# Two rows of 16 small-tile matmuls of a pair of batches formed as one row of 32, in a fused attention and mixture-of-experts kernel

## The chip, the cores and the metric

The kernel runs on one core of one Trainium2 chip. The metric is device time in microseconds of the whole launch, the median of several runs. Beside the runs there is one profiled execution, from which all views of the trace come.

## What is computed

There are 8 batches of 576 tokens with 8 heads of 64, 32 packed queries per head, 4 experts, a model width of 512 and a hidden width of 1024 per expert.

```python
p_packed = sm_attn(p, k, v)                      # 32 packed rows per head
out = sm_attn(q, p_packed, p_packed)             # tokens attend to the packed rows
x = out.transpose(0, 2, 1, 3).reshape(B * S, H * D)
for e in range(E):
    h = np.maximum(x @ w1[e], 0.0)
    result += prob[:, e:e + 1] * (h @ w2[e])     # prob: normalised domain probabilities
```

`sm_attn` is softmax attention with the scale 1/8.

## The kernel before

**Folding.** The attention output of a token is a weighted sum of 32 packed rows per head. So `x @ w1` is computed as (attention weights of the tokens) x (packed rows times `w1`). The second factor is the folded weight of a batch. A *chunk* is half an expert's hidden width (512 columns); there are 8 chunks. `g_form` (L286) folds a chunk for a pair of batches: its matmuls multiply `ppbd` (packed rows, 64x32) with `wraw` (the raw `w1`, 64x512) on small tiles of TensorE, which write different partitions of the same PSUM buffer. The four pairs of heads go as two *groups* g = 0, 1. One group of a pair of batches is 8 calls, which the trace shows as a row of 16 records on L76. `together` keeps such calls side by side in TensorE's queue. One PSUM buffer (`dbl`, two banks) takes one group: the first half for the even batch, the second for the odd one. Each half is then split in two parts of the tile `ghl`: ACT casts it to the high part (`hi_of`, L105), DVE subtracts that from PSUM for the low part (`lo_of`, L109).

**Units.** The main loop runs over 64 *units* u = (sweep, chunk, batch): 4 sweeps over pairs of batches, 8 chunks in each, two batches. (The second and third units change places, as do the two before the last.) So an even unit works on the even batch of a pair, an odd unit on the odd one, and each sweep has 16 units. A unit does seven *products* (`product`, L452: 12 matmuls `dbl<-st,tt`, a Strassen-like scheme for `h @ w2`), i = 0 to 6. Between them stand, behind i = 1, 3, 4 and 6 (the table `GROUPS`), the four groups of 12 matmuls with `ghl` (`mm1_groups`: `dbl<-xh,ghl` and `dbl<-xl,ghl`), which compute a quarter each of the next unit's hidden blocks. Their result leaves PSUM through DVE (L343, `ablk`). `s_operand` makes the Strassen sums of the blocks on DVE (L368, `sblk`) and splits them into `st` on ACT (L105) and POOL (L109). A product's result is added to `acc` by DVE (L470); in the first chunk ACT copies it (L468).

**Folding within the units.** An even unit u from 4 to 60 folds the *next* chunk for both batches of the pair. `g_form` is a generator: one step makes one group, and `next(gsteps, None)` is called behind products 3 and 6; in unit 60 (`AHEAD`) behind products 0 and 1. Units 0 to 3 fold in other ways; unit 3 already issues both groups without anything between. The raw weights of the chunk after are loaded behind an even unit (`w1_load`, four tiles `wraw`, four buffers).

**Other work.** In each sweep but the last the attention of the next pair (`pack_unit`, `tok_unit`: L172 to L269, among them `ppn`, L208) is cut into steps and laid between the products. In the first sweep, and only there, `t_form` also makes the seven Strassen operands `tt` of `w2` for the next chunk, with differences on POOL and DVE (L405, tiles `b` and `ablk`), and stores them. Later sweeps load `tt` back.

**Buffers.** PSUM has four buffers `dbl` for everything. `ghl` has five buffers in `gpool`; from the second sweep on the pool `glast` holds one more tile (`ghl6`), used once.

**What sets the order.** TensorE's order is that of the code within limits: a row that `together` makes stays whole, and matmuls before and after it don't cross it. All else, the order of each engine's queue and which buffer a tile gets, is decided by a scheduler that simulates the program. Each engine works through its queue in order, so an instruction that waits holds up all behind it.

Of the kernel before, what the change touches and what calls it, by code (L numbers as in the profile page):

```python
# [9 lines left out]
F32R = mybir.dt.float32r  # L10
# [6 lines left out]
P = 128  # L17
B, H, S, D = 8, 8, 576, 64
NPK = 32
E, DM, F = 4, 512, 1024  # L20
NPAIR = H // 2
NG = NPAIR // 2
SB = B // 2
HS = S // 2
FC = 512
NCH = E * F // FC
# [14 lines left out]
def attention_moe(ctx: ExitStack, tc: tile.TileContext, q, k, v, p, dp, w1, w2, out):  # L41
    nc = tc.nc
# [7 lines left out]
    gpool = pool("gpool")  # L50
# [33 lines left out]
    def dbl():  # L84
        return ps_dbl.tile([P, 2, 512], F32, name="dbl")
# [12 lines left out]
    def cols(b, hh):  # L98

        i = (hh + b) % 2  # L100
        return slice(i * NPK, (i + 1) * NPK)

    def hi_of(dst, src, eng):
        if eng is nc.scalar:
            return nc.scalar.copy(out=dst, in_=src)  # L105
        return eng.tensor_copy(out=dst, in_=src)

    def lo_of(dst, src, hi, eng):
        return eng.tensor_tensor(out=dst, in0=src, in1=hi.bitcast(F32), op=ALU.subtract)  # L109
# [173 lines left out]

    gs = {}

    def g_form(bs, ch, raws):  # L286

        for g in range(NG):
            ps = dbl()
            pss = {b: ps[:, b % 2] for b in bs}  # L290
            calls = []
            for hs in range(4):
                pr, hh = 2 * g + hs // 2, hs % 2
                rows = slice(hh * D, (hh + 1) * D)
                for b in bs:
                    c0 = (hs // 2) * 2 * NPK + cols(b, hh).start
                    calls.append(dict(
                        out=pss[b][c0:c0 + NPK, :], lhsT=ppbd[b % 4][rows, pr, cols(b, hh)], rhs=raws[pr][rows, :],
                        start=True, stop=True,
                    ))  # L300
            together(calls)
            for b in bs:
                if (b, ch, g) == (B - 1, NCH - 2, 0):
                    ghl = glast.tile([P, 2, FC], F32R, name="ghl6")
                else:
                    ghl = gpool.tile([P, 2, FC], F32R, name="ghl", bufs=5)
                hi_of(ghl[:, 0, :], pss[b], nc.scalar)
                marks[b, ch, g, "low"] = lo_of(ghl[:, 1, :], pss[b], ghl[:, 0, :], nc.vector).ins
                gs.setdefault((b, ch), []).append(ghl)
            yield  # L310

    units = [(sb, ch, 2 * sb + i) for sb in range(SB) for ch in range(NCH) for i in range(2)]
# [271 lines left out]
    nothing = iter(())  # L584
    GROUPS = {1: ((0, 0),), 3: ((0, 1),), 4: ((1, 1),), 6: ((1, 0),)}
    GROUPS_LAST = {1: ((0, 0),), 3: ((1, 0),), 4: ((0, 1),), 6: ((1, 1),)}
    GROUPS_LATE = {4: ((0, 0), (0, 1)), 5: ((1, 1),), 6: ((1, 0),)}
    AT_FIRST = ((4, pack_unit, 0), (7, pack_unit, 1), (9, tok_unit, 0), (12, tok_unit, 1))
    def second_tile(n):
# [16 lines left out]
    for u, (sb, ch, b) in enumerate(units):  # L606
        odd = b % 2 == 1
        nxt = units[u + 1] if u + 1 < len(units) else None

        step = 2 * ch + b % 2  # L610
        if sb + 1 < SB:
            pair = [2 * sb + 2, 2 * sb + 3]
            for at_step, make, g in AT_FIRST if sb == 0 else AT_LATER:
                if at_step == step:
                    drain(back)
                    back = make(pair, g, att_tile, relief=sb == 0)

        gsteps = nothing
        nsb, nch = (sb, ch + 1) if ch + 1 < NCH else (sb + 1, 0)
        if u == 0:  # L620
            gsteps = g_form([0], 1, raws)
        elif u == 2 or u == 3:
            gsteps = g_form([1] if u == 2 else [0, 1], u - 1, raws)
            drain(gsteps)
            raws = w1_load(u)
        elif 3 < u <= AHEAD and not odd and nsb < SB:
            gsteps = g_form([2 * nsb, 2 * nsb + 1], nch, raws)
        if u == 2 * NCH - 1:
            later.close()
            glast = later.enter_context(tc.tile_pool(name="glast", bufs=1, reuse_waits="tile"))  # L630
        elif u == LAST - 1:
            extra = plain_operand(NCH - 1)
            next(extra)
        elif u == LAST:
            for _ in combine(b, SUMS_LAST):
                pass
            for r in range(2):
                for n in range(2):
                    quadrant(r, n)
                    if r == 0:  # L640
                        s_operand(u, LA + n)
            break
        forming = u == 0 or u > 2 and odd and sb == 0 and ch + 1 < NCH
        if forming:
            tsteps = t_form(ch + 1, raw_tile, {"t1": nc.gpsimd, "t2": nc.vector, "t3": nc.vector, "t4": nc.gpsimd})
            next(tsteps)
        for i in range(NPROD):
            product(u, i)
            n = i + LA
            if n < NPROD:  # L650
                s_operand(u, n)
            elif nxt:
                s_operand(u + 1, n - NPROD)
            if nxt:
                for grp in (GROUPS_LATE if u in (1, AHEAD) else GROUPS_LAST if u == LAST - 1 else GROUPS).get(i, ()):
                    mm1_groups(u + 1, [grp])
            if u == 0:
                drain(gsteps)
            elif i in ((0, 1) if u == AHEAD else (3, 6)):
                next(gsteps, None)  # L660
            if u == 1 and i == 3:
                drain(second)
                drain(g_form([1], 0, raws))
                raws = w1_load(1)
            for _ in range(SECOND[u][i] if u in SECOND and i < len(SECOND[u]) else 0):
                next(second, None)
            if i == 4 and u > 1 and u + 2 < len(units) and units[u + 2][1] % 2 == 0:
                load_probs(units[u + 2][2], units[u + 2][1] // 2)
            if i % 2 == 0 or sb == 0 and step >= AT_FIRST[2][0]:
                next(back, None)  # L670
            if sb == 0 and i in (FORM_ODD if odd or u == 0 else FORM_EVEN):
                next(tsteps, None)
            next(sums, None)
            if sb == 0 and not odd:
                t_store(ch, i)
            if u == LAST - 1:
                if i == 1:
                    next(extra)
                elif i in (0, 5, 6):
                    t_load(nxt[1], i)  # L680
            elif nxt and not forming and nxt[1] != ch:
                t_load(nxt[1], i)
        drain(gsteps)
        drain(sums)
        if ch == NCH - 1:
            sums = combine(b, SUMS)
        if u == 0:
            raws = w1_load(0)
            load_probs(1, 0)
        elif not odd and u > 2:  # L690
            nsb, nch = (sb, ch + 2) if ch + 2 < NCH else (sb + 1, ch + 2 - NCH)
            if nsb < SB:
                raws = w1_load(nch)
# [34 lines left out]
```

## Time and profile before

| what | us |
| --- | --- |
| median of 3 runs | 1298.41 (1297.54 to 1298.51) |
| the profiled execution's own time | 1297.59 |
| its span in the trace | 1295.8 |
| first sweep with units 4 to 15, about | 120 to 360 |
| later three sweeps and the end, about | 360 to 1296 |

The engines are PE (TensorE's matmuls), PEld (its weight loads), DVE (VectorE), ACT (ScalarE), POOL (GpSimd) and SP (SyncE, which issues DMAs). A timeline row gives start and length in us, engine, line, operation, `out<-in` by the program's names, shapes, the number of instructions of the row, and in brackets the idle time ahead of it with what ended it. Matmuls are pipelined: a matmul starts while its predecessors still run, so lengths overlap and the time that PE's stream takes is read from start to start.

### The profile page before, as it was taken

To read this page: it belongs to the slowest core of one execution; us is meant where nothing else is said; L and a number is where in the kernel's file an instruction comes from. 1 tells how busy PE (TensorE), PEld (TensorE's weight loads), DVE (VectorE), ACT (ScalarE), POOL (GpSimd) and SP (SyncE) were. 2 spreads that over 40 slices of the span, in tenths; PEclk is the share of its full clock that TensorE was granted. 3 is DMA by queue.
4 is the path that set the end of the run, shared out by engine and by line. 5 is a ranking of instruction groups with operands and counts; after the bars stand their busy time and mean duration, and the time that the engine had idled before them with its cause. 6 is when DMAs were issued, how large, how long until landed. Compare 5 with 4: busy or idle time off the path is not lost.

```text
span 1295.8 us, 26890 instructions
## 1 busy us (share of the span) xinstructions
PE 1273.2 (98%) x10776; PEld 1178.4 (91%) x10776; DVE 951.5 (73%) x1304; ACT 495.2 (38%) x884; POOL 857.0 (66%) x570
## 2 busy tenths in 40 slices
PE   7899999999999999999999999999999999999998
PEld 4689999998999989999999999999999999999998
DVE  6786677899975666997686666789669466666676
ACT  3445545646334333333325433333333533333321
POOL 4778888798995544666577554476568655555565
PEclk9999999999999999999999999999999999999999
DMA  9885656544465543554444456433446443344562
GB/s 350 305 300 191 219 169 230 180 145 167 157 220 195 170 154 119 175 177 156 134 149 168 162 163 205 144 126 105 148 141 210 155 138 111 115 139 151 169 205 97
DMA packets 91707, 223.93 MB, mean 173 GB/s; under 512 B 9280, under 2 KB 32192, under 8 KB 91584
## 3 DMA queue, kind: packets, MB, share of 16 engines
q1 hardware_dynamic: 90768, 221.92, 51.4%
q8 instruction: 86, 1.41, 0.4%
q10 hardware_dynamic: 816, 0.30, 0.1%
q14 instruction: 37, 0.30, 0.1%
HBM read 183.31 MB, written 38.87 MB: 171 GB/s over the span
## 4 chain that ended last, share of the span: by engine, by line
PE 84%; POOL 7%; DVE 5%; issue 2%; DMA 1%; ACT 1%; SPq 0%; DVEq 0%; ACTq 0%; POOLq 0%
PE dbl L68 77%; PE dbl L76 6%; POOL st L109 4%; POOL tt L109 2%; DVE sblk L368 1%; POOL b L405 1%; PE dbl L71 1%; DMA xl<-in_q 1%; POOL acc L501 1%; DVE ablk L343 1%; DVE nb L172 0%; DVE a L264 0%; DVE acc L470 0%; ACT a L178 0%; POOL xl L109 0%
## 5 line engine op out<-in xcount | busy, mean ns | idle before, releaser
L68 PEld LDWEIGHTS dbl<-st,tt 128*128 128x128 f32 x5388 | 729.3, 188 | 59.2 <-POOL st L109 25.7
L68 PE MATMUL dbl<-st,tt 128*128 128x288 f32 x5388 | 773.4, 297 | 2.8 <-POOL st L109 1.9
L109 POOL TENSOR_TENSOR st<-sblk,st 128x576 fp32r<-128x576 f32 x252 | 392.5, 1565 | 204.6 <-ACT st L105 198.2
L68 PE MATMUL dbl<-xh,ghl 128*128 128x288 f32 x2048 | 416.7, 295 | 5.0 <-DVE ghl L109 2.7
L109 POOL TENSOR_TENSOR st<-ablk,st 128x576 fp32r<-128x576 f32 x193 | 289.7, 1505 | 181.4 <-ACT st L105 171.3
L470 DVE TENSOR_TENSOR acc<-dbl,acc 128x576 f32<-128x576 f32 x385 | 289.1, 753 | 115.6 <-PE dbl L68 114.6
L68 PEld LDWEIGHTS dbl<-xh,ghl 128*128 128x128 f32 x2048 | 328.4, 188 | 7.5 <-DVE ghl L109 4.1
L343 DVE SCALAR_TENSOR_TENSOR ablk<-dbl,pbt 128x576 f32<-128x576 f32 x256 | 192.5, 753 | 158.2 <-PE dbl L68 157.7
L68 PE MATMUL dbl<-xl,ghl 128*128 128x288 f32 x1024 | 300.9, 294 | 1.0 <-DVE xl L109 1.0
L105 ACT CAST st<-sblk 128x576 fp32r<-128x576 f32 x252 | 170.5, 677 | 283.5 <-DVE sblk L368 194.6
L105 ACT CAST st<-ablk 128x576 fp32r<-128x576 f32 x193 | 130.6, 677 | 224.3 <-PE dbl L68 202.3
L68 PEld LDWEIGHTS dbl<-xl,ghl 128*128 128x128 f32 x1024 | 192.1, 188 | 1.4 <-DVE xl L109 1.4
L105 ACT CAST ghl<-dbl 128x512 fp32r<-128x512 f32 x128 | 74.9, 587 | 146.5 <-PE dbl L76 87.8
L368 DVE TENSOR_TENSOR sblk<-ablk 128x576 f32<-128x576 f32 x126 | 122.0, 969 | 9.3
L109 DVE TENSOR_TENSOR ghl<-dbl,ghl 128x512 fp32r<-128x512 f32 x128 | 87.4, 685 | 11.1 <-ACT ghl L105 7.5
L76 PE MATMUL dbl<-wraw,ppbd 64*32 64x512 f32 x1024 | 74.7, 601 | 0.4 <-DMA wraw<-in_w 0.4
L368 DVE TENSOR_TENSOR sblk<-ablk,sblk 128x576 f32<-128x576 f32 x63 | 67.0, 1063 | 5.7
L109 POOL TENSOR_TENSOR tt<-b,tt 128x512 fp32r<-128x512 f32 x42 | 62.3, 1491 | 2.1 <-ACT tt L105 2.0
L368 DVE TENSOR_TENSOR sblk<-sblk,ablk 128x576 f32<-128x576 f32 x63 | 57.1, 907 | 1.7
L501 POOL TENSOR_TENSOR acc<-acc,acc 128x576 f32<-128x576 f32 x28 | 47.0, 1688 | 16.2 <-DVE acc L470 16.1
L468 ACT COPY acc<-dbl 128x576 f32<-128x576 f32 x56 | 35.9, 642 | 41.6 <-PE dbl L68 41.0
L501 DVE TENSOR_TENSOR acc<-acc,acc 128x576 f32<-128x576 f32 x28 | 40.8, 1462 | 5.0 <-POOL acc L501 4.6
(91 smaller groups left out, 433.2 us busy)
## 6 DMA issues: line engine op xcount, KB each, us to landing
tt<-td SPq DMA_DIRECT2D x192, 512.0 KB, 4.4
wraw<-in_w SPq DMA_DIRECT2D x136, 256.0 KB, 3.1
td<-tt SPq DMA_DIRECT2D x56, 512.0 KB, 3.7
pbt<-pnd SPq DMA_DIRECT2D x32, 288.0 KB, 4.4
out<-acc SPq DMA_DIRECT2D x31, 288.0 KB, 2.3
kt<-in_k SPq DMA_DIRECT2D x14, 576.0 KB, 5.7
kt<-in_q SPq DMA_DIRECT2D x14, 576.0 KB, 5.5
vt<-in_v SPq DMA_DIRECT2D x15, 512.0 KB, 5.6
```

The lines of the kernel that those rows point to most:

```text
L68: on_pe(nc.tensor.matmul(**kw))
L71: on_pe(nc.tensor.transpose(**kw))
L76: ins = nc.tensor.matmul(**kw).ins
L105: return nc.scalar.copy(out=dst, in_=src)
L109: return eng.tensor_tensor(out=dst, in0=src, in1=hi.bitcast(F32), op=ALU.subtract)
L343: nc.vector.scalar_tensor_tensor(out=a, in0=ps[:, :, 0:HS], scalar=0.0, in1=pbt[b][:, c * HS:(c + 1) * HS].rearrange("p (o t) -> p o t", o ...
L368: nc.vector.tensor_tensor(out=t, in0=blk(x), in1=blk(y), op=op)
L405: eng[m].tensor_tensor(out=blk[place], in0=blk[x], in1=blk[y], op=ALU.subtract)
L468: nc.scalar.copy(out=accs[b, i], in_=psv)
L470: nc.vector.tensor_tensor(out=accs[b, i], in0=psv, in1=accs[b, i], op=ALU.add)
L501: eng.tensor_tensor(out=m[dst], in0=m[x], in1=m[y], op=op)
```

## The change

`g_form` takes a list of groups of folding groups. In even units from 4 on, both groups go as one step: 16 calls (32 records) side by side, over two PSUM buffers, and only then the four evictions. In the first sweep the step stands behind product 6, where the `ghl` tiles of the chunk before have had their last use, so that five buffers do; the first group of the odd units there moves from behind product 1 to behind product 2 (`GROUPS_ODD`). In the later sweeps it stands behind product 3 and takes its tiles from a ring of six (`ghl_tile`, every sixth from `glast`). In unit 60 it stands behind product 0.

```diff
+    def ghl_tile():
+        n, ring["n"] = ring["n"], ring["n"] + 1
+        if n % 6 == 0:
+            return glast.tile([P, 2, FC], F32R, name="ghl6")
+        return gpool.tile([P, 2, FC], F32R, name="ghl", bufs=5)
+
+    def g_form(bs, ch, raws, rows=None, tile=lambda: gpool.tile([P, 2, FC], F32R, name="ghl", bufs=5)):
-        for g in range(NG):
-            ps = dbl()
-            pss = {b: ps[:, b % 2] for b in bs}
-            calls = []
-            for hs in range(4):
...
+        for gr in rows or [[g] for g in range(NG)]:
+            pss, calls = {}, []
+            for g in gr:
+                ps = dbl()
+                pss.update({(b, g): ps[:, b % 2] for b in bs})
+                for hs in range(4):
...
             together(calls)
             for b in bs:
-                if (b, ch, g) == (B - 1, NCH - 2, 0):
-                    ghl = glast.tile([P, 2, FC], F32R, name="ghl6")
-                else:
-                    ghl = gpool.tile([P, 2, FC], F32R, name="ghl", bufs=5)
-                hi_of(ghl[:, 0, :], pss[b], nc.scalar)
...
+                for g in gr:
+                    ghl = tile()
+                    hi_of(ghl[:, 0, :], pss[b, g], nc.scalar)
+                    marks[b, ch, g, "low"] = lo_of(ghl[:, 1, :], pss[b, g], ghl[:, 0, :], nc.vector).ins
+                    gs.setdefault((b, ch), []).append(ghl)
             yield
...
+    GROUPS_ODD = {2: ((0, 0),), 3: ((0, 1),), 4: ((1, 1),), 6: ((1, 0),)}
...
         elif 3 < u <= AHEAD and not odd and nsb < SB:
-            gsteps = g_form([2 * nsb, 2 * nsb + 1], nch, raws)
+            whole = dict(rows=[range(NG)])
+            if sb > 0:
+                whole["tile"] = ghl_tile
+            gsteps = g_form([2 * nsb, 2 * nsb + 1], nch, raws, **whole)
...
-                for grp in (GROUPS_LATE if u in (1, AHEAD) else GROUPS_LAST if u == LAST - 1 else GROUPS).get(i, ()):
+                for grp in (GROUPS_LATE if u in (1, AHEAD) else GROUPS_LAST if u == LAST - 1 else GROUPS_ODD if odd and sb == 0 else GROUPS).get(i, ()):
                     mm1_groups(u + 1, [grp])
...
-            elif i in ((0, 1) if u == AHEAD else (3, 6)):
+            elif i in ((0,) if u == AHEAD else (6,) if sb == 0 else (3, 6)):
                 next(gsteps, None)
```

Three places show how the engines' queues move.

First, TensorE in unit 18, a later sweep, in the difference of the two queues around product 3 (`xh` and `xl` are the attention weights' high and low parts; a number behind a name is the buffer):

```order
 L76 MATMUL dbl<-wraw,ppbd_85 32x512
 L76 MATMUL dbl<-wraw,ppbd_86 32x512
+L76 MATMUL dbl<-wraw,ppbd_85 32x512
+L76 MATMUL dbl<-wraw,ppbd_86 32x512
+L76 MATMUL dbl<-wraw,ppbd_85 32x512
+L76 MATMUL dbl<-wraw,ppbd_86 32x512
+L76 MATMUL dbl<-wraw,ppbd_85 32x512
+L76 MATMUL dbl<-wraw,ppbd_86 32x512
+L76 MATMUL dbl<-wraw,ppbd_85 32x512
+L76 MATMUL dbl<-wraw,ppbd_86 32x512
 L68 MATMUL dbl<-st,tt 128x288 x12
 L68 MATMUL dbl<-xh_3082,ghl 128x288 x2
```

The second group's eight calls now stand directly behind the first group's; the same eight are gone from their place behind product 6.

Second, DVE in unit 52, a plain unit of the last sweep, around product 3. Before (the first group only; the second follows further on):

```order
L343 SCALAR_TENSOR_TENSOR ablk<-dbl,pbt 128x576
L368 TENSOR_TENSOR sblk<-ablk 128x576
L109 TENSOR_TENSOR ghl<-dbl,ghl 128x512
L470 TENSOR_TENSOR acc_12595<-dbl,acc_12595 128x576
L109 TENSOR_TENSOR ghl<-dbl,ghl 128x512
L343 SCALAR_TENSOR_TENSOR ablk<-dbl,pbt 128x576
```

After (line numbers are 7 higher, so L343, L368 and L470 are L350, L375 and L477):

```order
L350 SCALAR_TENSOR_TENSOR ablk<-dbl,pbt 128x576
L375 TENSOR_TENSOR sblk<-ablk 128x576
L109 TENSOR_TENSOR ghl_13442<-dbl,ghl_13442 128x512
L109 TENSOR_TENSOR ghl<-dbl,ghl 128x512 x2
L477 TENSOR_TENSOR acc_12595<-dbl,acc_12595 128x576
L109 TENSOR_TENSOR ghl<-dbl,ghl 128x512
L350 SCALAR_TENSOR_TENSOR ablk<-dbl,pbt 128x576
```

Three low parts now stand in a row ahead of the product's sum, and the fourth behind it.

Third, DVE at the end of unit 10, in the first sweep. Before:

```order
L368 TENSOR_TENSOR sblk<-ablk,sblk 128x576
L109 TENSOR_TENSOR ghl<-dbl,ghl 128x512
L405 TENSOR_TENSOR ablk<-b_3601,ablk 128x512
L470 TENSOR_TENSOR acc_1214<-dbl,acc_1214 128x576
L109 TENSOR_TENSOR ghl<-dbl,ghl 128x512
L470 TENSOR_TENSOR acc_1236<-dbl,acc_1236 128x576
L343 SCALAR_TENSOR_TENSOR ablk<-dbl,pbt 128x576
```

After (L405 is L412):

```order
L375 TENSOR_TENSOR sblk<-ablk,sblk 128x576
L109 TENSOR_TENSOR ghl<-dbl,ghl 128x512
L412 TENSOR_TENSOR ablk<-b_3601,ablk 128x512
L109 TENSOR_TENSOR ghl<-dbl,ghl 128x512 x2
L477 TENSOR_TENSOR acc_1214<-dbl,acc_1214 128x576
L477 TENSOR_TENSOR acc_1236<-dbl,acc_1236 128x576
L109 TENSOR_TENSOR ghl<-dbl,ghl 128x512
```

The difference `ablk<-b` of the second weights, which waits for POOL's `b`, keeps its place behind the first low part; two more low parts now stand behind it, and the fourth behind two sums.

More of the change, by code (lines that the diff above doesn't have):

```diff
@@ L284, in attention_moe @@
     gs = {}
-    def g_form(bs, ch, raws):
-        for g in range(NG):
-            ps = dbl()
-            pss = {b: ps[:, b % 2] for b in bs}
-            calls = []
-            for hs in range(4):
[L293 to L300, printed above, removed]
+    ring = {"n": 0}
@@ new lines, in ghl_tile @@
+    def ghl_tile():
[10 more added lines that the diff above has]
+                for hs in range(4):
+                    pr, hh = 2 * g + hs // 2, hs % 2
+                    part = slice(hh * D, (hh + 1) * D)
+                    for b in bs:
+                        c0 = (hs // 2) * 2 * NPK + cols(b, hh).start
+                        calls.append(dict(
+                            out=pss[b, g][c0:c0 + NPK, :], lhsT=ppbd[b % 4][part, pr, cols(b, hh)],
+                            rhs=raws[pr][part, :], start=True, stop=True,
+                        ))
@@ L301, in g_form @@
             together(calls)
             for b in bs:
-                if (b, ch, g) == (B - 1, NCH - 2, 0):
-                    ghl = glast.tile([P, 2, FC], F32R, name="ghl6")
-                else:
-                    ghl = gpool.tile([P, 2, FC], F32R, name="ghl", bufs=5)
-                hi_of(ghl[:, 0, :], pss[b], nc.scalar)
-                marks[b, ch, g, "low"] = lo_of(ghl[:, 1, :], pss[b], ghl[:, 0, :], nc.vector).ins
-                gs.setdefault((b, ch), []).append(ghl)
+                for g in gr:
[3 more added lines that the diff above has]
+                    gs.setdefault((b, ch), []).append(ghl)
```

## The prediction

> **What bounds the kernel now.** I read three views in this order: the page's busy shares, the chain that ended last, and the busy time by stretch. In the first two, look at PE's share.
>
> ```profile
> PE 1273.2 (98%) x10776; PEld 1178.4 (91%) x10776; DVE 951.5 (73%) x1304; ACT 495.2 (38%) x884; POOL 857.0 (66%) x570
> ...
> PE 84%; POOL 7%; DVE 5%; issue 2%; DMA 1%; ACT 1%; SPq 0%; DVEq 0%; ACTq 0%; POOLq 0%
> ```
>
> PE works 1273.2 of 1295.8 us, and 84% of the chain lies on it. An average hides stages, so the third view splits the span where the first sweep over the weight chunks ends (columns: length, busy time and count of each engine, PEclk, DMA share, GB/s).
>
> ```profile
> 120.00:360.00 240.00, 235.14 (x2062) 216.75 (x2061) 200.21 (x251) 117.92 (x269) 211.89 (x140) 1.00 0.52 177
> 360.00:1268.00 908.00, 907.74 (x7585) 851.65 (x7584) 652.14 (x905) 319.57 (x515) 549.23 (x363) 1.00 0.49 158
> ```
>
> In the three later sweeps PE lacks 0.26 of 908 us: whatever shortens its instruction stream shortens the kernel, until some wait appears. In the first sweep PE lacks 4.86 of 240 us, while DVE (200.2, 83%) and POOL (211.9, 88%) are nearly full: there the other engines end some waits, and work that moves on DVE or ACT can cost time. The granted clock is 1.00 in both.
>
> **What one row of folding costs on PE.** The next rows are from PE's timeline at unit 52 (start, length, form, count); the lengths are pipelined, so I use starts only.
>
> ```profile
> 1082.33 0.29 PE L68 MATMUL dbl<-xl,ghl 128*128 128x288 f32 x1
> 1082.55 1.09 PE L76 MATMUL dbl<-wraw,ppbd 64*32 64x512 f32 x16
> 1083.57 1.86 PE L68 MATMUL dbl<-st,tt 128*128 128x288 f32 x12
> 1085.27 0.43 PE L68 MATMUL dbl<-xh,ghl 128*128 128x288 f32 x2
> ...
> 1086.87 3.36 PE L68 MATMUL dbl<-st,tt 128*128 128x288 f32 x24
> 1090.07 0.43 PE L68 MATMUL dbl<-xh,ghl 128*128 128x288 f32 x2
> ...
> 1091.52 0.29 PE L68 MATMUL dbl<-xl,ghl 128*128 128x288 f32 x1
> 1091.74 1.09 PE L76 MATMUL dbl<-wraw,ppbd 64*32 64x512 f32 x16
> 1092.76 2.52 PE L68 MATMUL dbl<-st,tt 128*128 128x288 f32 x17
> ```
>
> Plain matmuls start every 0.133 us (24 in 1090.07 - 1086.87 = 3.20). From the last plain start before a row of 16 to the first one after it pass 1083.57 - 1082.33 = 1.24 us, and 1092.76 - 1091.52 = 1.24 for the second row. The 12 matmuls behind a row take 1085.27 - 1083.57 = 1.70 rather than 1.60. So one row costs 1.24 - 0.13 + 0.10 = 1.21 us, two 2.42.
>
> Once the kernel already runs a row of 32, in unit 3:
>
> ```profile
> 108.45 0.29 PE L68 MATMUL dbl<-xl,ghl 128*128 128x288 f32 x1
> 108.66 1.95 PE L76 MATMUL dbl<-wraw,ppbd 64*32 64x512 f32 x32
> 110.54 3.46 PE L68 MATMUL dbl<-st,tt 128*128 128x288 f32 x24
> 114.31 0.54 PE L68 MATMUL dbl<-xh,ghl 128*128 128x288 f32 x2 [0.31 <-DVE ghl L109]
> ```
>
> Here 110.54 - 108.45 = 2.09 pass, and the length of the 24 behind it is 3.46, again 0.10 over the 3.36 above. It costs 2.09 - 0.13 + 0.10 = 2.06. Entering and leaving the small tiles is paid once instead of twice, and a merge saves 2.42 - 2.06 = **0.36 us**. It is made in 29 even units: 6 in the first sweep (units 4 to 14), 23 later. All of it lies on PE, so it counts in full where no wait answers: 23 x 0.36 = 8.3 us in the later sweeps, 6 x 0.36 = 2.2 in the first.
>
> The last row above also shows the danger: behind that row of 32, PE waited 0.31 us for a folded tile's low part. The matmuls get faster to issue, but four halves must now leave PSUM behind one row rather than two.
>
> **Evictions in the later sweeps.** DVE and ACT around the row at T = 1082.55:
>
> ```profile
> 1083.52 0.76 DVE L368 TENSOR_TENSOR sblk<-ablk 128x576 f32<-128x576 f32 x1
> 1084.39 0.69 DVE L109 TENSOR_TENSOR ghl<-dbl,ghl 128x512 fp32r<-128x512 f32 x1
> 1085.46 0.76 DVE L470 TENSOR_TENSOR acc<-dbl,acc 128x576 f32<-128x576 f32 x1 [0.38 <-PE dbl L68]
> ```
>
> ```profile
> 1083.77 0.59 ACT L105 CAST ghl<-dbl 128x512 fp32r<-128x512 f32 x1 [1.99 <-PE dbl L76]
> 1085.12 0.59 ACT L105 CAST ghl<-dbl 128x512 fp32r<-128x512 f32 x1 [0.76 <-DVE ghl L109]
> ```
>
> The first half's cast starts at T+1.22, its low part on DVE at T+1.84. Call the halves e0, e1 (even batch, groups 0 and 1) and o0, o1 (odd batch). Group 0's records come first in the new row, so e0 keeps these times: low from T+1.84 to T+2.5. The cast of e1 can run beside that (group 1 is done at about T+2.0), its low ends at T+3.3; o0's cast waits only for e0's low, and its low follows at T+4.1. Then DVE does the product's sum (0.76), and o1's low ends near T+5.5. The order of DVE's rows agrees: three low parts, a sum, the fourth. PE needs o0's PSUM buffer again for the product after next: the row ends 0.85 later than now, the product takes 1.70, twelve group matmuls 1.60, so at T + 1.02 + 0.85 + 1.70 + 1.60 = T+5.2. Spare time 1.1 us; o1's buffer and the tile itself are needed later still. I charge nothing for this in a plain unit. Some later units carry attention work on DVE, and where two pieces of 0.76 stand ahead of o0's low, PE waits 2 x 0.76 - 1.1 = 0.4: I take **+0.4** once, since PE's lack there is 0.26 us now, with 0 and 23 x 0.31 = 7.1 (the wait behind the existing row of 32, in every unit) as the ends.
>
> [...]
>
> **The first sweep.** Here the row moves from the fourth to behind the seventh product, and DVE and ACT serve attention and the second weights too. Units 4 and 6 I cost like the later ones: 2 x -0.36 = -0.7.
>
> Unit 8, around its second row at T = 232.39:
>
> ```profile
> 233.61 0.59 ACT L105 CAST ghl<-dbl 128x512 fp32r<-128x512 f32 x1 [1.97 <-PE dbl L76]
> 234.38 0.31 ACT L208 ACTIVATE ppn<-dbl,rs 128x64 f32<-128x64 f32 x1 [0.18 <-PE dbl L68]
> ```
>
> ```profile
> 234.91 0.68 DVE L109 TENSOR_TENSOR ghl<-dbl,ghl 128x512 fp32r<-128x512 f32 x1
> ```
>
> ```profile
> 234.75 0.30 PE L71 MATMUL dbl<-ident,ppn 128*64 128x128 f32 x1 [0.43 <-ACT ppn L208]
> ```
>
> ACT's queue will hold three casts ahead of ppn. The third (o0) waits for e0's low, which ends at 235.59 = T+3.2; cast to T+3.8, ppn to T+4.1, and the transpose starts at about T+4.15. PE would be there 0.43 before its present start at T+2.36, plus 0.85 for the longer row: T+2.8. The wait grows from 0.43 to about 1.3: +0.8 -0.36 = +0.4.
>
> Unit 10, the page's DVE, POOL and PE rows behind its second row at 272.65:
>
> ```profile
> 276.19 0.68 DVE L109 TENSOR_TENSOR ghl<-dbl,ghl 128x512 fp32r<-128x512 f32 x1
> 277.46 0.69 DVE L405 TENSOR_TENSOR ablk<-b,ablk 128x512 f32<-128x512 f32 x1 [0.59 <-POOL b L405]
> ...
> 278.73 0.68 DVE L109 TENSOR_TENSOR ghl<-dbl,ghl 128x512 fp32r<-128x512 f32 x1
> ```
>
> ```profile
> 275.61 1.81 POOL L405 TENSOR_TENSOR b<-ablk,b 128x512 f32<-128x512 f32 x1
> ```
>
> ```profile
> 276.96 0.43 PE L68 MATMUL dbl<-xh,ghl 128*128 128x288 f32 x2
> ...
> 278.96 3.43 PE L68 MATMUL dbl<-st,tt 128*128 128x288 f32 x24 [0.26 <-DVE acc L470]
> ```
>
> In the new order DVE does e0's low, then the subtraction that waits for POOL's b, and only then e1 and o0. POOL ends b at 277.42 whatever PE does (its queue is full). So: subtraction to 278.1, e1 to 278.75, o0 to 279.4. The third product of unit 11, which takes o0's buffer, starts there, with its twelve group matmuls behind it rather than ahead: 279.4 + 1.6 + 1.6 = 282.6, where now the same work ends at 278.96 + 1.6 = 280.6. **+2.0**, the merge's gain included.
>
> Units 12 and 14:
>
> ```profile
> 316.61 1.83 DVE L264 TENSOR_TENSOR a<-a,s 128x576 f32<-128x576 f32 x1
> 318.36 0.68 DVE L109 TENSOR_TENSOR ghl<-dbl,ghl 128x512 fp32r<-128x512 f32 x1
> ```
>
> ```profile
> 319.10 0.40 PE L68 MATMUL dbl<-xh,ghl 128*128 128x288 f32 x1 [1.72 <-DVE ghl L109]
> ...
> 358.97 0.40 PE L68 MATMUL dbl<-xh,ghl 128*128 128x288 f32 x1 [0.64 <-DVE ghl L109]
> ```
>
> PE already waits 1.72 us because an attention product (1.83) stands ahead of a low part on DVE. All four lows now stand behind it, with o0's about two pieces later (321.0), and the third product with them: +2.4 by the same sum as in unit 10, less 0.36 for unit 14's merge. Part comes back, since POOL and DVE catch up during the wait and later ones, the 0.64 among them, shrink or go: I take half, +1.0 for both units.
>
> First sweep: -0.7 + 0.4 + 2.0 + 1.0 = **+2.7 us**, with ends at -2.2 (every wait hidden) and +5.5 (nothing comes back, and unit 8 or 10 spills on).
>
> **The rest.** All four weight loads are issued behind the row instead of two and two; the page has
>
> ```profile
> wraw<-in_w SPq DMA_DIRECT2D x136, 256.0 KB, 3.1
> ```
>
> 3.1 us to land, and the row that needs them stands two units, 14 products of 1.6 us or at least 22 us, further on: nothing, and still nothing if SP's few stores behind them slip. The sixth buffer of the later sweeps adds no instruction. The first group of odd units in the first sweep moves one product later with the same matmuls; its only price is counted in units 10 and 12.
>
> **Sum.** -8.3 + 0.4 + 2.7 = -5.2 us against the profiled execution's own 1297.59 us, which is 0.8 below the median of 1298.41: **1292.4 us**.
>
> **Rivals.**
> - *A, the first sweep hides its waits.* For: it has 4.86 us of idle PE, and a wait absorbs another. Against: DVE's fixed order behind POOL's b. First sweep -2.2 to 0, sum -10.5 to -8.3: 1287.1 to 1289.3.
> - *B, the first sweep loses more.* For: DVE at 83%, POOL at 88%, and a late low part delays blocks, their st operands on POOL and the next products. First sweep +5 to +7.5, sum -3 to -0.5: 1294.6 to 1297.1.
> [...]
> - *D, the row of 32 splits or pays the mode twice*: 1297.59 + 2.7, about 1300. PE's new order has 16 calls with nothing between them, so I give it next to nothing.
>
> **Chances.** Forecast (first sweep +0.5 to +5, later ones -8.3 to -7.5: 1289.8 to 1295.1) 0.52, A 0.25, B 0.18, C and D 0.05. The range runs from A's lower end to the middle of B: 1287.2 to 1296.0. A gain or loss counts from 0.2%, 2.6 us, about what a measurement of this kernel can tell from no change. The forecast, A and the first sixth of B (a sum of -3 to -2.6) are faster: 0.80. The rest of B is the same: 0.15. C and D: 0.05 slower.
>
> **What would show it.** PE's timeline must have rows of 32 with 2.09 us from start to start, 29 of them, and no row of 16 behind unit 2; the stretch of the later sweeps should be 8 us shorter with PE's lack still under 0.6 us. The chain's waits for ghl should stand in units 8, 10 and 12 alone. The forecast is wrong if PE waits for ghl or for a low part's PSUM buffer behind the rows of the later sweeps, or if the first sweep ends earlier than now.

## The result: slower

The changed kernel takes 1309.98 us (median of 5 runs, 1308.14 to 1310.43), the kernel before 1298.21 (5 runs, 1297.54 to 1298.51). The ratio is 1.0092, with a 95% interval from 1.0081 to 1.0103. The profiled execution of the changed kernel took 1308.14 us, its span is 1306.3. The forecast was 1292.4 with 0.05 for slower.

The changed kernel's page, the busy shares and the chain that ended last, against those of before:

```profile
PE 1267.4 (97%) x10776; PEld 1184.3 (91%) x10776; DVE 953.2 (73%) x1304; ACT 493.6 (38%) x884; POOL 857.9 (66%) x570
...
PE 82%; DVE 7%; DMA 4%; POOL 3%; issue 1%; ACT 1%; SPq 0%; DVEq 0%; ACTq 0%; POOLq 0%
```

PE is busy 5.8 us less for the same 10776 matmuls, yet the span is 10.5 us longer: time was saved on PE, and more than that was put back as waiting. DVE's share of the chain rose from 5% to 7% and that of DMA from 1% to 4%, while POOL's fell from 7% to 3%.

**Where it went.** Each unit has 84 matmuls `dbl<-st,tt`, so the start of the matmul 84 x u of that form is the start of unit u in both timelines. Differences between the two kernels, in us:

| start of unit | before | changed | difference | gained or lost since the row above |
| --- | --- | --- | --- | --- |
| 4 | 128.77 | 128.94 | +0.17 | |
| 8 | 211.81 | 214.25 | +2.44 | +2.27 |
| 10 | 253.79 | 256.76 | +2.96 | +0.52 |
| 11 | 273.67 | 277.59 | +3.92 | +0.96 |
| 12 | 291.81 | 301.96 | +10.15 | +6.23 |
| 16 | 372.58 | 386.11 | +13.53 | +3.38 |
| 63 | 1278.66 | 1289.15 | +10.49 | -3.04 |

The busy time by stretch says the same. Before, first sweep (units 4 to 15) and later sweeps (units 16 to 62):

```profile
128.77:372.58 243.81, 238.95 (x2091) 220.56 (x2089) 204.62 (x254) 117.48 (x267) 213.67 (x142) 1.00 0.55 187
372.58:1278.66 906.08, 905.50 (x7567) 849.18 (x7565) 650.36 (x902) 318.22 (x512) 549.34 (x362) 1.00 0.48 154
```

The same two stretches in the changed kernel:

```profile
128.94:386.11 257.17, 240.62 (x2090) 225.13 (x2089) 205.12 (x255) 117.72 (x268) 212.07 (x142) 0.98 0.52 179
386.11:1289.15 903.04, 899.21 (x7566) 851.97 (x7565) 652.30 (x901) 316.55 (x512) 551.61 (x362) 1.00 0.48 155
```

In the first sweep PE now lacks 257.17 - 240.62 = 16.6 us instead of 4.9, and the granted clock is 0.98 where it was 1.00. In the later ones PE's work fell by 6.3 us, but its lack rose from 0.6 to 3.8.

The row itself costs what was forecast. PE's timeline in a plain later unit of the changed kernel:

```profile
1094.48 0.29 PE L68 MATMUL dbl<-xl,ghl 128*128 128x288 f32 x1
1094.70 1.95 PE L76 MATMUL dbl<-wraw,ppbd 64*32 64x512 f32 x32
1096.58 1.60 PE L68 MATMUL dbl<-st,tt 128*128 128x288 f32 x10
```

1096.58 - 1094.48 = 2.10 us, against 2.09 in the forecast; a plain pair of units is 0.33 us shorter than before.

**The two large waits.** PE at the end of unit 10, changed kernel:

```profile
275.72 1.95 PE L76 MATMUL dbl<-wraw,ppbd 64*32 64x512 f32 x32
277.59 3.46 PE L68 MATMUL dbl<-st,tt 128*128 128x288 f32 x24
285.04 3.22 PE L68 MATMUL dbl<-st,tt 128*128 128x288 f32 x12 [3.99 <-DVE ghl L109]
```

The third product of unit 11 wants the PSUM buffer of the row's first group, and waits 3.99 us for the low part of o0 (the first group's half for the odd batch), the last that is read from that buffer. DVE and POOL there:

```profile
279.19 0.68 DVE L109 TENSOR_TENSOR ghl<-dbl,ghl 128x512 fp32r<-128x512 f32 x1
281.82 1.87 DVE L412 TENSOR_TENSOR ablk<-b,ablk 128x512 f32<-128x512 f32 x1 [1.96 <-POOL b L412]
283.62 1.28 DVE L109 TENSOR_TENSOR ghl<-dbl,ghl 128x512 fp32r<-128x512 f32 x2
```

```profile
280.51 1.28 POOL L412 TENSOR_TENSOR b<-ablk,b 128x512 f32<-128x512 f32 x1
281.74 1.41 POOL L109 TENSOR_TENSOR st<-ablk,st 128x576 fp32r<-128x576 f32 x1
```

The first low part is done at 279.87. Then DVE stands before the second weights' difference until POOL has made `b` at 281.79, and that difference takes 1.87 us instead of the 0.69 of before, with POOL at work beside it. Only at 283.62 come the next two low parts, those of e1 and o0; PE waits for the second. The matmuls behind the wait are slow as well (granted clock in the eighth column):

```profile
285.04:290.78 5.74, 5.74 (x24) 5.74 (x25) 2.54 (x4) 1.64 (x3) 4.69 (x4) 0.52 0.45 183
```

24 matmuls take 5.74 us, 0.24 each, where 24 take 3.20 elsewhere: a granted clock of 0.52. At the end of unit 12 PE stands 3.87 us behind o0's low part in the same way. There a piece of DVE's attention work (L264) stands ahead of the first low parts, and a difference ahead of o0's:

```profile
325.63 1.96 DVE L264 TENSOR_TENSOR a<-a,s 128x576 f32<-128x576 f32 x1
327.51 1.27 DVE L109 TENSOR_TENSOR ghl<-dbl,ghl 128x512 fp32r<-128x512 f32 x2
328.71 0.68 DVE L412 TENSOR_TENSOR ablk<-b,ablk 128x512 f32<-128x512 f32 x1
329.31 0.68 DVE L109 TENSOR_TENSOR ghl<-dbl,ghl 128x512 fp32r<-128x512 f32 x1
```

```profile
330.13 2.08 PE L68 MATMUL dbl<-st,tt 128*128 128x288 f32 x12 [3.87 <-DVE ghl L109]
```

### The profile page after: what moved, and what is told of

It reads as the page before. It is cut to its first block, busy times and chain, and to the rows that moved or that the text cites. A ratio compares the mean times of both kernels' runs of the same rounds, so it can differ in the third digit from the quotient of the medians.

```text
span 1306.3 us, 26905 instructions
## 1 busy us (share of the span) xinstructions
PE 1267.4 (97%) x10776; PEld 1184.3 (91%) x10776; DVE 953.2 (73%) x1304; ACT 493.6 (38%) x884; POOL 857.9 (66%) x570
## 4 chain that ended last, share of the span: by engine, by line
PE 82%; DVE 7%; DMA 4%; POOL 3%; issue 1%; ACT 1%; SPq 0%; DVEq 0%; ACTq 0%; POOLq 0%
PE dbl L68 77%; PE dbl L76 5%; DVE sblk L375 2%; POOL st L109 2%; DVE ablk L350 1%; DVE ghl L109 1%; DMA xh<-in_q 1%; DVE acc L477 1%; DMA b<-in_w 1%; POOL acc L508 1%; DMA xl<-in_q 1%; DMA pnd<-pb 1%; PE dbl L71 1%; DMA pbt<-pnd 1%; POOL tt L109 1%
## 5 line engine op out<-in xcount | busy, mean ns | idle before, releaser
L68 PE MATMUL dbl<-st,tt 128*128 128x288 f32 x5388 | 774.4, 297 | 16.6 <-DVE ghl L109 9.5
L477 DVE TENSOR_TENSOR acc<-dbl,acc 128x576 f32<-128x576 f32 x385 | 288.3, 752 | 116.7 <-PE dbl L68 116.5
L350 DVE SCALAR_TENSOR_TENSOR ablk<-dbl,pbt 128x576 f32<-128x576 f32 x256 | 192.5, 753 | 164.0 <-PE dbl L68 161.0
L375 DVE TENSOR_TENSOR sblk<-ablk 128x576 f32<-128x576 f32 x126 | 124.2, 986 | 9.3
L375 DVE TENSOR_TENSOR sblk<-ablk,sblk 128x576 f32<-128x576 f32 x63 | 66.5, 1055 | 6.0 <-POOL st L109 0.5
L76 PE MATMUL dbl<-wraw,ppbd 64*32 64x512 f32 x1024 | 67.7, 595 | 0.0
L375 DVE TENSOR_TENSOR sblk<-sblk,ablk 128x576 f32<-128x576 f32 x63 | 57.4, 911 | 1.7
L508 DVE TENSOR_TENSOR acc<-acc,acc 128x576 f32<-128x576 f32 x28 | 37.9, 1360 | 5.0 <-POOL acc L508 4.6
```

The costliest lines, as they stand in the source:

```text
L68: on_pe(nc.tensor.matmul(**kw))
L76: ins = nc.tensor.matmul(**kw).ins
L350: nc.vector.scalar_tensor_tensor(out=a, in0=ps[:, :, 0:HS], scalar=0.0, in1=pbt[b][:, c * HS:(c + 1) * HS].rearrange("p (o t) -> p o t", o ...
L375: nc.vector.tensor_tensor(out=t, in0=blk(x), in1=blk(y), op=op)
L477: nc.vector.tensor_tensor(out=accs[b, i], in0=psv, in1=accs[b, i], op=ALU.add)
L508: eng.tensor_tensor(out=m[dst], in0=m[x], in1=m[y], op=op)
```

## The experiments

Theory 1: the loss is made in the first sweep, where the four low parts stand in DVE's queue behind work that waits for others. Theory 2: emptying four halves behind one row costs everywhere. Theory 3: the late first group of the odd units makes the loss. All kernels are compared with the kernel before on the same chip; its medians there were 1297.19 (e1, e2, e3, e6), 1297.70 (e7 to e10) and 1297.37 (e11 to e13).

### e1 and e2: one part of the run at a time

e1, the later sweeps alone, against the changed kernel:

```diff
-            whole = dict(rows=[range(NG)])
-            if sb > 0:
-                whole["tile"] = ghl_tile
+            whole = dict(rows=[range(NG)], tile=ghl_tile) if sb > 0 else {}
...
-            elif i in ((0,) if u == AHEAD else (6,) if sb == 0 else (3, 6)):
+            elif i in ((0,) if u == AHEAD else (3, 6)):
```

`GROUPS_ODD` is not used in it, so the odd units are as before.

> Only the later sweeps and unit 60 have the row of 32; the first sweep is as before. Matched at the starts of the units, the changed kernel is 13.5 us behind at unit 16 and 10.5 us behind at the end, so the later sweeps gave 3.0. Theory 1 (the loss is made in the first sweep alone): about 1298.2 - 3.0 = 1295, between 1293 and 1297. [...] Theory 3 (the late first group of the odd units makes the loss): like theory 1 here.

e2, the first sweep alone (the tile `ghl6` goes where the kernel before has it, in e3 too):

```diff
-            whole = dict(rows=[range(NG)])
-            if sb > 0:
-                whole["tile"] = ghl_tile
+            whole = dict(rows=[range(NG)]) if sb == 0 else {}
...
-            elif i in ((0,) if u == AHEAD else (6,) if sb == 0 else (3, 6)):
+            elif i in ((0, 1) if u == AHEAD else (6,) if sb == 0 else (3, 6)):
```

> Only the first sweep has the row of 32, behind product 6, with the late first group; the later sweeps are as before. Theory 1 and theory 3: about 1298.2 + 13.5 = 1311.7, between 1308 and 1314. Theory 2: the 11.8 us of loss are spread over 29 rows, so 6 of them bring about 2.4 and the time is near 1300.6.

e1: 1294.08 us (10 runs, 1293.58 to 1295.29), ratio 0.9975 (0.9965 to 0.9984). e2: 1312.15 (4 runs, 1310.55 to 1313.11), ratio 1.0114 (1.0099 to 1.0129). Theory 2 falls: the first sweep brings the whole loss, the 23 rows of the later ones a gain. e1 is faster than both kernels. e2 changes three things in the first sweep: the rows are merged, they stand behind product 6, and the first group of the odd units is late. The third is taken apart below; two rows of 16 that both stand behind product 6 were not tried, so the first two are not told apart there.

### e3: the late group alone

```diff
-            whole = dict(rows=[range(NG)]) if sb == 0 else {}
+            whole = {}
...
-            elif i in ((0, 1) if u == AHEAD else (6,) if sb == 0 else (3, 6)):
+            elif i in ((0, 1) if u == AHEAD else (3, 6)):
```

(against e2; `GROUPS_ODD` stays.)

> Only the first group of the odd units of the first sweep moves from behind product 1 to behind product 2; all rows are of 16 and stand where they stood. Theory 1 (the four evictions behind product 6 make the loss): within 2 us of 1298.2. Theory 3 (the late group makes it, since the next unit's blocks come a product later): 1305 or more.

1301.50 us (6 runs, 1300.48 to 1302.49), ratio 1.0032 (1.0020 to 1.0044). Neither theory had it: between the two. Matched unit starts give +2.4 us over the first sweep, +1.2 in unit 6 and +1.2 in unit 10. By the medians of the whole run it is +4.3. The late group, which the prediction priced at nothing, thus costs 2.4 to 4.3 us alone, where e2 lost 13.5 by its unit starts and 15.0 by its medians: 18 to 29% of the loss.

### e6, e9 and e11: the order on DVE, and the group

e6 puts the second weights' differences on DVE behind the four low parts:

```diff
-                eng[m].tensor_tensor(out=blk[place], in0=blk[x], in1=blk[y], op=ALU.subtract)
+                ins = eng[m].tensor_tensor(out=blk[place], in0=blk[x], in1=blk[y], op=ALU.subtract).ins
+                if eng[m] is nc.vector and ch >= 3:
+                    for b, g in [(b, g) for b in range(2) for g in range(NG)]:
+                        after(ins, marks[b, ch, g, "low"])
```

> The changed kernel with one order more: in the first sweep, the differences of the second weights that DVE does (L412 there) stand behind all four low parts. In the changed kernel TensorE waits 3.99 us at 285.04 for a low part that stands behind such a difference, and the matmuls behind it run at 0.24 us for another 2.3 us. Theory 1 in its narrow form (that difference, which waits for POOL, holds the low part): the wait at the start of unit 11 falls below 1.5 us with no slow matmuls behind it, so about 5 us off: 1305. The rival (DVE is late there anyhow, whatever stands ahead): the wait stays above 3 us and the time within 2 us of 1310.

1298.48 us (8 runs, 1297.09 to 1301.29), ratio 1.0013 (1.0002 to 1.0023): more than expected. DVE's and PE's rows at the end of unit 10 in e6:

```profile
275.99 2.02 DVE L109 TENSOR_TENSOR ghl<-dbl,ghl 128x512 fp32r<-128x512 f32 x3
277.93 0.75 DVE L480 TENSOR_TENSOR acc<-dbl,acc 128x576 f32<-128x576 f32 x1
278.60 0.68 DVE L109 TENSOR_TENSOR ghl<-dbl,ghl 128x512 fp32r<-128x512 f32 x1
279.19 1.36 DVE L412 TENSOR_TENSOR ablk<-b,ablk 128x512 f32<-128x512 f32 x1
```

```profile
278.16 1.83 PE L68 MATMUL dbl<-st,tt 128*128 128x288 f32 x12 [0.30 <-DVE ghl L109]
```

The wait of 3.99 us is 0.30, with no slow matmul behind it, and DVE doesn't wait for POOL at all. At the end of unit 12 only part is cured: of 3.87 us 2.53 are left, since L264 still stands ahead of the low parts there. Another 2.5 us come from unit 6 (by matched unit starts it lost 1.4 us in the changed kernel and gains 1.1 in e6). There, in the changed kernel, ACT's queue holds a cast that waits for a load of the second weights ahead of `ppn`:

```profile
174.12 0.62 ACT L105 CAST tt<-b 128x512 fp32r<-128x512 f32 x1 [4.33 <-DMA b<-in_w]
174.64 0.31 ACT L208 ACTIVATE ppn<-dbl,rs 128x64 f32<-128x64 f32 x1
```

```profile
175.00 0.30 PE L71 MATMUL dbl<-ident,ppn 128*64 128x128 f32 x1 [2.23 <-ACT ppn L208]
```

The kernel before has the same order, but its load lands 1.95 us sooner, and PE waits 0.51 us there:

```profile
172.17 0.62 ACT L105 CAST tt<-b 128x512 fp32r<-128x512 f32 x1 [2.36 <-DMA b<-in_w]
```

The merged rows with the odd units as before (e11, below: 2.05 us) and the late group alone (e3: 1.71 us) each bring a long wait there. In e6 the scheduler has the two the other way round:

```profile
170.66 0.31 ACT L208 ACTIVATE ppn<-dbl,rs 128x64 f32<-128x64 f32 x1
172.98 0.62 ACT L105 CAST tt<-b 128x512 fp32r<-128x512 f32 x1 [2.01 <-DMA b<-in_w]
```

So one order more on DVE changed another on ACT, and 2.5 us of e6's gain are of this second kind.

e9 is e6, and e11 the changed kernel, each with the first group of the odd units back in its place:

```diff
-                for grp in (GROUPS_LATE if u in (1, AHEAD) else GROUPS_LAST if u == LAST - 1 else GROUPS_ODD if odd and sb == 0 else GROUPS).get(i, ()):
+                for grp in (GROUPS_LATE if u in (1, AHEAD) else GROUPS_LAST if u == LAST - 1 else GROUPS).get(i, ()):
```

> The changed kernel with the four low parts ahead of the second weights' differences on DVE, as in e6 (1298.48), and with the first group of the odd units back behind product 1. If the late first group costs what it cost alone (matched unit starts: +1.2 in unit 6 and +1.2 in unit 10), the time is about 2.4 lower than e6's: 1296. If the group behind product 1 waits for its tile in this place, which the late group was to avoid, TensorE waits for ghl there in units 5 to 15 and the time is above 1298.5.

> The changed kernel with the first group of the odd units back behind product 1; the order on DVE is left to itself, so that this is the fourth corner beside the changed kernel (late group), e6 (late group, low parts first) and e9 (old group, low parts first). If order and group add up: the changed kernel less e6 minus e9, 2.6 us, so about 1307 against 1310. If the late group was what kept the wait at the start of unit 11 down, it is 1310 or more; if the scheduler orders DVE otherwise here, the wait at the start of unit 11 is under 1.5 us and the time below 1302.

e9: 1295.86 us (8 runs, 1295.35 to 1297.93), ratio 0.9989 (0.9978 to 0.9999), as expected, though by its trace only unit 10 gives back what the late group cost (1.3 us); in unit 6 e6 had gained it already. e11: 1305.25 us (2 runs, 1304.66 and 1305.84), ratio 1.0061 (1.0041 to 1.0082), a little below what was expected. What the first sweep (units 4 to 15) lost against the kernel before, by matched unit starts:

| | DVE's order left to the scheduler | low parts ahead of the differences |
| --- | --- | --- |
| first group late | +13.4 (changed kernel) | +3.6 (e6) |
| first group in its old place | +9.5 (e11) | +2.1 (e9) |

The order is worth 7 to 10 us, of which 2.3 to 2.5 come from unit 6 and so from ACT's order; the late group is worth 1.5 to 4. With both undone the six rows behind product 6 still cost 2.1 us, although PE's own work is 6 x 0.33 = 2.0 less: there are waits left in units 8, 13 and 15.

### e7 and e13: the half clock

Product 1 of units 11 and 13, right ahead of the two large waits, is computed twice (e7) or three times (e13) into the same buffer:

```diff
-        for j in range(2):
+        for j in (0, 1, 0, 1) if u in (11, 13) and i == 1 else (0, 1):
```

> The changed kernel with product 1 of units 11 and 13 computed twice in the same buffer (24 matmuls instead of 12 there, 1.6 us more work each). In the changed kernel TensorE stands still for 3.99 and 3.87 us right behind these two products, and the next 22 and 16 matmuls start every 0.24 us instead of 0.13, which costs 2.3 and 1.6 us. Theory (TensorE runs at half clock because it stood still about 4 us): the waits shrink to about 2.4 us, end at the same time, and the slow matmuls go: 3.9 us less, 1306 against 1310. Rival (the slow matmuls come from what ends the wait, or from a busy DVE and POOL): they stay, and the time is 1310 or more.

> As e7, with product 1 of units 11 and 13 computed three times (24 matmuls, 3.2 us, more than in the changed kernel). In e7 the wait of 2.47 us was still followed by 15 slow matmuls (1.56 us), that of 2.32 us by none. Theory (half clock follows a stand of about 2.6 us from start to start and more): the waits fall to about 0.9 us, no matmul there takes 0.24 us, and the time is about 1.5 less than e7's: 1307. Rival (the slow matmuls come with the place): 15 or more slow matmuls behind the wait at 285.

e7: 1308.24 us (2 runs, 1307.35 and 1309.13), ratio 1.0081 (1.0061 to 1.0101). e13: 1307.48 (2 runs, 1306.89 and 1308.07), ratio 1.0079 (1.0058 to 1.0099). The places in e7:

```profile
285.01 1.96 PE L68 MATMUL dbl<-st,tt 128*128 128x288 f32 x12 [2.47 <-DVE ghl L109]
...
329.19 1.83 PE L68 MATMUL dbl<-st,tt 128*128 128x288 f32 x12 [2.31 <-DVE ghl L109]
```

and the first of them in e13:

```profile
286.00 1.83 PE L68 MATMUL dbl<-st,tt 128*128 128x288 f32 x12 [0.89 <-DVE ghl L109]
```

The waits end when they ended, since nothing ahead of the low parts changed. Behind 2.47 us 15 matmuls at 0.24 remain (1.56 us too long, where it was 2.3), behind 2.31 and 0.89 none. At the first place the slow matmuls go with the length of the stand: 22 behind 3.99 us, 15 behind 2.47, none behind 0.89. So the place alone does not bring them. A gain in time is not shown: the medians rest on two runs each, and their ratios differ from the changed kernel's 1.0092 by less than their intervals are wide. By the traces, PE, sooner through here, meets a new wait for POOL's `st` at 350 (1.70 us in e7; 2.53 in e13; the mean granted clock of the two profiled executions is 0.999 and 0.997).

### e8, e10 and e12: what the later sweeps still lose

e8 and e12 are e1 with the later sweeps' row behind product 0 and behind product 6:

```diff
-            elif i in ((0,) if u == AHEAD else (3, 6)):
+            elif i in ((3, 6) if sb == 0 else (0,)):
```

```diff
-            elif i in ((0,) if u == AHEAD else (3, 6)):
+            elif i in ((0,) if u == AHEAD else (3, 6) if sb == 0 else (6,)):
```

e10 is e1 with two rows in the three units that wait longest:

```diff
-            whole = dict(rows=[range(NG)], tile=ghl_tile) if sb > 0 else {}
+            whole = dict(rows=[[0], [1]] if u in (32, 36, 48) else [range(NG)], tile=ghl_tile) if sb > 0 else {}
```

> As e1 (first sweep as before, later sweeps merged: 1294.08), but the row of 32 of the later sweeps stands behind product 0 instead of product 3. In e1 the later sweeps lose 4.4 us to waits that the old kernel has for 0.9 only, most of them in units 32, 36 and 48 (0.64, 1.05, 1.28), where DVE is late around product 3 to 6. Theory (a place where DVE is late makes these waits, so another place changes them): the time moves by over 1 us either way; at best all 23 merges pay in full, 0.33 each, and it is near 1297.2 - 7.6 = 1290. Rival (the waits follow from four halves behind one row, wherever it stands): within 1 us of 1294.

> As e1, but units 32, 36 and 48 keep two rows of 16 behind products 3 and 6. Theory (the merge itself makes the waits of 0.64, 1.05 and 1.28 there): they fall to the old kernel's 0, 0.27 and 0, three merges of 0.33 are given up: 2.7 - 1.0 = 1.7 us less than e1, 1292.4. Rival (the waits come from the new order of the whole sweep, not from these rows): they stay, and the time is 1 us above e1.

> As e1, but the row of 32 of the later sweeps stands behind product 6, where in the first sweep it does harm, and the first group of the odd units stays behind product 1. Theory (a row of 32 does harm where DVE's queue holds something that waits for POOL or attention work ahead of the low parts; in the later sweeps nothing of the second weights is there): the plain units lose nothing and the time is 1291 to 1296. Rival (the place behind product 6 itself does harm, since two products and a group ask for the buffers at once): TensorE waits for ghl in each later even unit and the time is above 1299.

e8: 1309.13 us (4 runs, 1308.30 to 1310.70), ratio 1.0086 (1.0069 to 1.0103), as slow as the changed kernel, with the first sweep untouched. Behind product 0 the row meets DVE's attention work; DVE and PE in unit 24 of e8:

```profile
538.60 1.98 DVE L264 TENSOR_TENSOR a<-a,s 128x576 f32<-128x576 f32 x1
540.51 0.77 DVE L269 STREAM_TRANSPOSE at<-a 128x576 f32<-128x576 f32 x1
541.20 1.25 DVE L109 TENSOR_TENSOR ghl<-dbl,ghl 128x512 fp32r<-128x512 f32 x2
542.38 0.73 DVE L477 TENSOR_TENSOR acc<-dbl,acc 128x576 f32<-128x576 f32 x1
```

```profile
543.21 4.94 PE L68 MATMUL dbl<-st,tt 128*128 128x288 f32 x24 [2.38 <-issue]
```

Two pieces, 2.7 us, stand ahead of the second and third low part, and a product's sum behind these. PE stands 2.38 us, and the 24 matmuls behind the wait take 4.78 us from start to start instead of 3.20. The profile names no releaser ("issue"); PE starts 0.10 us after the end of that sum, so it most likely waits for the sum's buffer.

e12: 1293.80 us (9 runs, 1292.87 to 1295.61), ratio 0.9973 (0.9963 to 0.9983). Behind product 6, where the row does harm in the first sweep, it gains in the later ones: 4.5 us by matched unit starts (e1: 3.2). So the place by itself is not the cause. The two places where PE still waits for a low part fit theory 1. They are the ends of units 30 and 46, where DVE has a final sum that waits for POOL ahead of the low parts. PE and DVE at the first of them:

```profile
672.55 0.53 PE L68 MATMUL dbl<-xh,ghl 128*128 128x288 f32 x2 [1.22 <-DVE ghl L109]
```

```profile
666.67 1.97 DVE L508 TENSOR_TENSOR acc<-acc,acc 128x576 f32<-128x576 f32 x1 [0.65 <-POOL acc L508]
```

e10: 1294.43 us (9 runs, 1294.21 to 1294.82), ratio 0.9975 (0.9966 to 0.9985), the same as e1. The wait in unit 36 is gone, those at the starts of units 32 and 48 stand unchanged, though no merged row is near. They are 0.64 and 1.29 us, counted from start to start less the usual 0.133; a row's bracket counts from the end of the matmul before and gives 0.16 less. In e1, PE and DVE at the start of unit 48:

```profile
1000.87 3.29 PE L68 MATMUL dbl<-st,tt 128*128 128x288 f32 x23 [1.13 <-issue]
```

```profile
998.13 1.97 DVE L508 TENSOR_TENSOR acc<-acc,acc 128x576 f32<-128x576 f32 x1 [0.66 <-POOL acc L508]
1000.03 0.74 DVE L350 SCALAR_TENSOR_TENSOR ablk<-dbl,pbt 128x576 f32<-128x576 f32 x1
```

and DVE at the same place before:

```profile
999.66 1.97 DVE L501 TENSOR_TENSOR acc<-acc,acc 128x576 f32<-128x576 f32 x1 [0.67 <-POOL acc L501]
1001.56 0.74 DVE L343 SCALAR_TENSOR_TENSOR ablk<-dbl,pbt 128x576 f32<-128x576 f32 x1
```

DVE's order is the same in both: the final sums of the pair wait for POOL, and the eviction of a block group that frees PE's next buffer stands behind them. PE waits there because it has got ahead, not because DVE got slower. That reading comes from the two traces; keeping two rows in the units before was not tried.

## Why the prediction was wrong, by its own steps

- **Cost of the row: right.** 2.10 us from start to start, 0.33 per merge.
- **Evictions in plain later units: right.** There is no wait behind their rows. But the term of +0.4 for all other later units was too small: of 23 x 0.33 = 7.6 us 3.0 were left, so 4.6 went to waits. The largest, in units 36 and 48, are 1.05 and 1.29 us, counted as above. The one at unit 48 lies where PE overtakes DVE and POOL, so the step "all of it lies on PE, so it counts in full" fails there.
- **Units 4 and 6: forecast -0.7, measured +2.3.** They were costed "like the later ones", although the second weights are loaded and cast there. The wait for `ppn`, which grew from 0.51 to 2.23 us, was not foreseen.
- **The late first group: priced at nothing beside units 10 and 12**, because the number of matmuls stays the same. Alone it cost 2.4 us by the trace.
- **Unit 8: right.** Forecast +0.4, measured +0.52, with a wait of 1.32 us where about 1.3 was worked out.
- **Unit 10: forecast +2.0, measured +7.2 to the start of unit 12.** This is the step that failed. The mechanism was named (a low part behind a difference that waits for POOL's `b`). The step that mis-sized it was "POOL ends b at 277.42 whatever PE does (its queue is full)". In the run `b` ended 4.4 us later, at 281.79. POOL worked without a pause from 249.71 to 283.15, so its queue was full, but it came into this stretch 4.69 us later than before (245.02):

```profile
245.08 3.93 ACT L248 ACTIVATE a<-a,m 128x32 f32<-128x32 f32 x18
...
249.02 0.61 ACT L105 CAST tt<-b 128x512 fp32r<-128x512 f32 x1
```

```profile
249.71 1.30 POOL L109 TENSOR_TENSOR tt<-b,tt 128x512 fp32r<-128x512 f32 x1 [2.53 <-ACT tt L105]
```

Of the 4.69 us, 2.96 are PE's own lateness at the start of unit 10, where the forecast had it 0.3 us early. The other 1.7 arise in unit 9: DVE makes a difference `b` at 245.90, behind attention work that it stood ahead of before (242.88), and ACT casts it to `tt` behind 18 exponentials, where before it did so ahead of them, at 243.60. With the late group alone (e3) POOL is also 1.7 us later than PE here, without it (e11) it is not, so this part belongs to the group that was priced at nothing. Then the difference on DVE took 1.87 us rather than 0.69, and 2.3 us of half clock came on top; the prediction had neither.
- **Units 12 and 14: forecast +1.0, measured +3.4**, in the same queue on DVE. That half of the wait would come back ("I take half") was a guess without a row.
- **Slower had 0.05.** PE's pace is set by o0's low part where DVE puts further pieces ahead of it: in the first sweep PE stood 3.99 and 3.87 us for it. In the later sweeps the prediction worked out 1.1 us of slack, and 3.0 us were gained. In the first sweep it reckoned with such pieces, but with their times held as they were. Rival B stopped at +7.5 for the first sweep; it was 13.4.

Whether the wait of 0.31 us behind the row of unit 3 comes from emptying four halves behind one row was not tried. The loss does not come from that alone: with the same casts and low parts the first sweep lost 13.4 us in the changed kernel and 3.6 in e6, and the later sweeps gained 3.2 in e1. What decided was the order in the queues that they stand in.

## What to carry to other kernels

When two bursts of work are merged, look at the queues of the engines that empty them: what stands between the first and the last eviction, and whether any of it waits for a third engine. Here one order more on DVE (e6) brought back 9.8 of 13.4 us, 2.5 of them through an order that the scheduler then changed on ACT. The times of an engine whose queue is full may not be held fixed: POOL stayed full and was still 4.4 us late. And a merge that pays in plain stages is best made there alone: e1 is 0.25% faster (0.16 to 0.35%) than the kernel before.

## What the runs showed of the hardware

Some of PE's stands were followed by matmuls that start every 0.24 us, others by matmuls at 0.133 us as elsewhere. What followed these seven (the stand is the idle time in the row's bracket):

| kernel, end of the stand | stand, us | matmuls behind it |
| --- | --- | --- |
| changed, 285.04 | 3.99 | 22 at 0.24 us |
| changed, 330.13 | 3.87 | ten at about 0.133 us, then 14 at 0.24 |
| e7, 285.01 | 2.47 | 15 at 0.24 us |
| e8, 543.21 | 2.38 | 24 in 4.78 us instead of 3.20 |
| e7, 329.19 | 2.31 | at about 0.133 us |
| changed, 175.00 | 2.23 | at about 0.133 us |
| e13, 286.00 | 0.89 | at about 0.133 us |

So a stand of about 4 us, the length that the theory of e7 went by, was not needed: 2.47 us brought 15 slow matmuls.

In the changed kernel's trace, between the start-up phase and the end of the last sweep, the granted clock changes at 283.74, 290.57, 331.52 and 334.93 us. The distances are 6.83, 40.96 and 3.41 us, that is 2, 12 and 1 times 3.413. Five stretches of that length, laid along these changes (length and PE's busy time follow the stretch, the granted clock is in the eighth column):

```profile
280.33:283.74 3.41, 0.72 (x6) 0.48 (x4) 1.92 (x2) 0.74 (x3) 2.82 (x3) 1.00 0.86 281
283.74:287.15 3.41, 2.11 (x9) 2.14 (x10) 3.08 (x5) 2.26 (x4) 2.73 (x3) 0.50 0.20 82
...
324.70:328.11 3.41, 1.56 (x12) 1.33 (x10) 3.41 (x4) 1.06 (x2) 2.01 (x2) 1.00 0.51 181
328.11:331.52 3.41, 1.39 (x10) 1.42 (x11) 3.41 (x7) 3.29 (x6) 1.47 (x2) 1.00 0.00 0
331.52:334.93 3.41, 3.41 (x17) 3.41 (x16) 1.72 (x3) 1.32 (x3) 3.41 (x3) 0.50 0.40 159
```

PE is idle for 2.69 us of the first stretch, and the next one is at half clock. The stand at the end of unit 12 covers two stretches: 1.85 us idle in the third row left the clock at 1.00, 2.02 in the fourth halved it. Among all such stretches of the changed kernel at full clock from 45 us to the end of the last sweep, these two, with 2.69 and 2.02 us, are the only ones followed by half clock; the next largest idle times, 1.85 and 1.73 us, were followed by 1.00. So in this trace the idle time within one stretch tells the cases apart: 2.02 of 3.41 us, 59%, went with half clock, and 1.85, 54%, did not.

The difference on DVE that took 1.87 instead of 0.69 us began at 281.82, just behind POOL's st at 281.74, and ended at 283.69, 0.54 us behind that one's end at 283.15. The five other differences of the changed kernel that began well inside a POOL instruction (at 53.95, 159.23, 202.11, 245.90 and 337.39) ended 0.54 to 0.55 us behind its end as well, and took 1.29 to 1.90 us. The eight remaining ones on DVE took 0.68 to 0.69; seven of them began while POOL ran nothing, one 0.02 us ahead of the end of a POOL instruction. What holds the six up until POOL is done was not shown.
